# An attention and MLP kernel on one core: batch 0 begun as 512 tokens instead of 256, v cast while it is loaded, and new gates between the two load queues

## The chip, the core and the metric

The kernel runs on one core of a Trainium2 chip. The metric is the device time of one execution in microseconds (us), lower is better. TensorE is called PE here (PEld is its loading of weights), VectorE DVE, ScalarE ACT, GpSimd POOL and SyncE SP. SP and POOL each issue loads and stores of their own queue; a load issued from POOL may change the type on its way (float32 in memory, bfloat16 in SBUF), a load issued from SP does not in this kernel.

## What is computed

Windowed attention with four sink tokens over 4 batches, 8 heads, 768 tokens and 64 elements a head, and behind it two dense layers with a squared ReLU between them:

```python
scores = scale * np.matmul(q, k.transpose(0, 1, 3, 2))
keep = is_sink | in_window            # first 4 tokens, or the last 128 up to one's own
a = softmax(np.where(keep, scores, -1e9))
x = np.matmul(a, v)                   # to [3072 tokens, 512]
h = np.maximum(x @ w_in, 0.0)         # 512 -> 2048
out = (h * h) @ w_out                 # 2048 -> 512
```

Inputs and output are float32; the kernel's matmuls take bfloat16.

## The kernel before, in words

Tokens go in tiles of 128 (six a batch) and slabs of 256 (three a batch). A batch passes through these steps:

- **Loads.** For batches 0 and 1, q and k come over SP's queue as float32 (line 345, tile `qr`), are cast and put in order by `regroup` (lines 208 and 210, tile `qs`, on DVE, POOL or ACT), transposed on PE (line 477, into the PSUM tile `pt`) and copied to `qkT` by DVE and ACT (lines 208 and 206). v comes over SP's queue as float32 (line 361, tile `vf`) and is cast by DVE or POOL (lines 208 and 210, into `v`). For batches 2 and 3 (`NATURAL`) POOL's queue loads q, k (line 378, tile `qn`) and v (line 388) with the cast in the load, and SP's queue transposes q and k by DMA (line 434).
- **Attention by slab.** PE makes the scores of a pair of heads (line 580, into `ps`), ACT takes the exponential (line 599, into `expm`), DVE multiplies by a mask (line 608), PE multiplies with v and with the sinks' v (line 641, into `po`; `es` and `vs` are the sinks' part), DVE divides (lines 652 and 653, into `xn_sb`). In the first 512 tokens of batch 0 the mask is instead added on PE as a bias before the scores (line 573), since the masks are not built yet.
- **The bridge.** For batches 0 and 1 PE turns x (line 678, into `px`) and ACT or DVE copies it to `xT`; for 2 and 3 a DMA does it (line 664).
- **Layer 1** (`layer1`): 16 matmuls of 128x256 or 8 of 128x512 are one operation (line 701, into `pm`), ACT takes the ReLU (line 710), DVE squares (line 717, into `gT`). **Layer 2** (`layer2`): four matmuls an operation (line 741, into `py`), then a copy (line 206) and a store (line 757).

`w_in` (line 300) and `w_out` (line 307) come in four parts each over POOL's queue, cast in the load.

What stands in which order on each engine isn't written out by hand. The class `Plan` gets every operation with its engines, a cost, what it waits for and a key; it keeps a model of the engines, the pools and the two queues, and takes again and again the operation that can start first (ties by key). `attention` and `layer1`/`layer2` set the keys: `at(g, f0, f1, pools)` spreads the operations of one group of tokens over the stretch f0 to f1 of a batch, `LO` and `HI` do so for batches 2 and 3. `PE_SLACK` and the `margin` of a DMA are corrections of that model. The order that comes out is what runs; the chip's engines then wait for each other by semaphores alone. PSUM holds two pools of two tiles, `att` and `den`.

`GROUPS` tells how many tokens of a batch are loaded and turned together. Before, batch 0 is begun with 256 tokens, then 256, then 256; each load is two pairs of heads (four heads) with rows of 512 bytes. Batch 1 has 512 and 256.

Loads of a queue are chained in the order of the calls at lines 784 to 811. A call's argument `behind` makes the load wait until a load of the other queue has landed (`after_dma`, a semaphore wait on the issuing engine). Before: `w_in` waits for a k load of the second 256 tokens (line 794); the loads of batch 0's third slab wait for `w_out(0)` (line 799); `w_out(2)` waits for v of that slab (line 801); batch 1's loads wait for `w_out(2)` (line 805); the first load of batch 2 waits for a v load of batch 1 (line 382).

While PE has nothing to do at the start, `warm` fills its gaps with matmuls of the identity (line 201).

Of the kernel before, what the change touches and what calls it, by code (L numbers as in the profile page):

```python
# [17 lines left out]
PE_SLACK = 0.219  # L18
# [115 lines left out]
def kernel(  # L134
# [28 lines left out]
    sizes = dict(att=2, den=2, qr=5, qs=6, vf=3, expm=8, r=3, osb=2)  # L163
# [149 lines left out]
    qr_slot, qs_slot, vf_slot = {}, {}, {}  # L313
    qn_t, qn_slot = {}, {}
    qr_t, qs_t, vf_t, ex_t, bank_t = {}, {}, {}, {}, {}
# [3 lines left out]
    GROUPS[0] = [(0, 2), (256, 2), (512, 2)]  # L319
# [3 lines left out]
    def load_qk(b, m0, ti, g, behind=None, yields=()):  # L323


        t0, n = GROUPS[b][g]
        if b == 0 and g < 2:
            half, share = g, (b, m0, ti)
        elif n == 2:
            half, share = m0 // 2, (b, "last", ti)  # L330
        else:
            half, share = None, (b, m0, ti)
        if not half:
            qr_slot[share] = Slot("qr", 2)
        qr_slot[b, m0, ti, g] = qr_slot[share]

        def run(e):
            if half is not None:
                if half == 0:
                    qr_t[share] = work["qr"].tile([128, 2, 4, n * D], FP32, name="qr", tag="qr")  # L340
                t = qr_t[share][:, half]
            else:
                t = work["qr"].tile([128, 4, n * D], FP32, name="qr", tag="qr")
            qr_t[b, m0, ti, g] = t
            return [nc.sync.dma_start(  # L345
                out=t,
                in_=(q, k)[ti][b, 2 * m0:2 * m0 + 4, t0:t0 + 128 * n, :].rearrange(
                    "h (p t) d -> p h (t d)", t=n))]
        ops["qk", b, m0, ti, g] = dma_op("sp", ("qk", b, m0, ti, g), run, 32 * ROW[256 * n], behind,
                                         () if half else [qr_slot[share]], yields)  # L350

    def load_v(b, s, behind=None, yields=()):

        sl = vf_slot[b, s] = Slot("vf", 1)
        for i in range(2):
            t = 2 * s + i

            def run(e, i=i, t=t):
                if i == 0:
                    vf_t[b, s] = work["vf"].tile([128, 2, H, D], FP32, name="vf", tag="vf")  # L360
                return [nc.sync.dma_start(
                    out=vf_t[b, s][:, i], in_=v[b, :, 128 * t:128 * t + 128, :].rearrange("h p d -> p h d"))]
            dma_op("sp", ("v", b, t), run, 8 * 8 * ROW[256], behind if i == 0 else None,
                   [sl] if i == 0 else (), yields)

    def load_natural(b, s, older_values):

        begun = [ops["layer1", b - 2, 0, 0], w_out_op[3]]
        for ti in (1, 0):
            if s == 0:  # L370
                qn_slot[b, ti] = Slot("qr", NT)
            for i in range(2):
                t = 2 * s + i

                def run(e, t=t, ti=ti):
                    if t == 0:
                        qn_t[b, ti] = work["qr"].tile([128, NT, DM], BF16, name="qn", tag="qr")
                    return [nc.gpsimd.dma_start(  # L378
                        out=qn_t[b, ti][:, t, :].rearrange("p (h d) -> p h d", d=D),
                        in_=(q, k)[ti][b, :, 128 * t:128 * t + 128, :].rearrange("h p d -> p h d"))]  # L380
                o = dma_op("pool", ("qk", b, ti, t), run, 64 * 0.032,
                           ("v", 1, 3) if (b, ti, t) == (2, 1, 0) else None,
                           [qn_slot[b, ti]] if t == 0 else ())
                o.after += begun
                o.margin = 2.229
        for t in (2 * s, 2 * s + 1):
            def run(e, t=t):
                return [nc.gpsimd.dma_start(  # L388
                    out=v_sb[b % 2][:, t, :, 0:D],
                    in_=v[b, :, 128 * t:128 * t + 128, :].rearrange("h p d -> p h d"))]  # L390
            o = dma_op("pool", ("v", b, t), run, 64 * 0.032)
            o.after += begun + older_values
            o.margin = 2.229
# [6 lines left out]
    def attention(b, key):  # L400
# [16 lines left out]
        def stage(g, f0, f1, side):  # L417
# [9 lines left out]
            if b in NATURAL:  # L427
                for s in range(NS):
                    for ti in (1, 0):
                        for i in range(2):  # L430
# [8 lines left out]
                            ops["turn", b, ti, t].margin = 4.81  # L439
# [3 lines left out]
            for m in range(0, NP, w) if b not in NATURAL else ():  # L443
                f = 0.08 * m
                m0 = m - m % 2
                bs = Slot(side, 2)
                regs = []
                for ti in (1, 0):
                    sl = qs_slot[b, m, ti, g] = Slot("qs", 1)

                    def regroup(e, m=m, m0=m0, ti=ti):
                        t = qs_t[b, m, ti, g] = work["qs"].tile([128, w, n, 2, D], BF16, name="qs", tag="qs")
                        r = qr_t[b, m0, ti, g][:, 2 * (m - m0):2 * (m - m0) + 2 * w, :]
                        if w == 2:
                            copy(e, t, r.rearrange("p (m h) (t d) -> p m t h d", m=2, d=D))
                        else:
                            copy(e, t[:, 0], r.rearrange("p h (t d) -> p t h d", d=D))
                    who = {"pool": 0.17 + w * n * 0.11}
                    if b or g < 2:
                        who["dve"] = 0.06 + w * n * 0.094  # L460
                    if b == 0 and g == 0:
                        who["act"] = 0.2 + w * n * 0.107
                    regs.append(op(at(f), who, regroup,
                                   after=[ops["qk", b, m0, ti, g]] + prev_tr + begun, takes=[sl],
                                   reads=[qr_slot[b, m0, ti, g]]))
# [38 lines left out]

            for s in range(t0 // 256, last // 256) if b not in NATURAL else ():
                def cast(e, s=s):
                    copy(e, vb[:, 2 * s:2 * s + 2, :, 0:D], vf_t.pop((b, s)))
                ops["cast", b, s] = op(at(0.3 + 0.5 * (256 * s - t0) / (last - t0)),
                                       {"pool": 1.08, "dve": 0.75} if g < 2 else {"pool": 1.08}, cast,
                                       after=[ops["v", b, 2 * s], ops["v", b, 2 * s + 1], c_sinks] + older_values + begun,  # L510
                                       reads=[vf_slot[b, s]])


            if g == 0:
# [7 lines left out]
                def sink_values(e):  # L522
                    for j in range(NP):
# [5 lines left out]
                A["sink_values"] = op(at(0.36), {"pool": 1.4, "dve": 0.9}, sink_values,  # L529
                                      after=older_values + [c_fill, c_sinks, ops["vs_in", b]])  # L530
# [23 lines left out]
            biased = b == 0 and g < 2  # L554
            for s in range(t0 // 256, last // 256):
                fs = 0.36 + 0.5 * (256 * s - t0) / (last - t0)
                norms = []
                for m0 in (0, 2):
# [4 lines left out]
                    def scores(e, ms, s=s, m0=m0, banks=banks):  # L563
# [32 lines left out]
                    for j, m in enumerate((m0, m0 + 1)):  # L596
# [19 lines left out]
                        if biased:  # L616
                            masked.append(ex)
                            continue
                        masked.append(op(at(fm + 0.03), {"pool": 1.3, "dve": 0.7} if s else {"dve": 0.58, "pool": 1.1},
                                         domask, after=[ex, late["masks"]]))  # L620
# [40 lines left out]
                if b in NATURAL:  # L661
                    for t in (2 * s, 2 * s + 1):
# [5 lines left out]
                        o_.margin = 3.168  # L668
# [115 lines left out]
    NATURAL = (2, 3)  # L784
    load_sinks("act", 0)
    for g, m0 in ((0, 0), (0, 2), (1, 0), (1, 2)):
        for ti in (1, 0):
            load_qk(0, m0, ti, g)
        if g:
            load_v(0, m0 // 2)  # L790
    for b in range(1, B):
        load_sinks("sp", b)
    for i in range(4):
        load_w_in(i, ("qk", 0, 2, 1, 1) if i == 0 else None)
    load_w_out(0)
    load_w_out(1)
    for m0 in (0, 2):
        for ti in (1, 0):
            load_qk(0, m0, ti, 2, ("w_out", 0) if m0 == 0 and ti == 1 else None, [("w_out", 1)])
    load_v(0, 2, None, ())  # L800
    load_w_out(2, ("v", 0, 4), [("v", 0, 5)])
    load_w_out(3, None, ())
    for m0 in (0, 2):
        for ti in (1, 0):
            load_qk(1, m0, ti, 0, ("w_out", 2) if m0 == 0 and ti == 1 else None, [("w_out", 3)])
    for m0 in (0, 2):
        for ti in (1, 0):
            load_qk(1, m0, ti, 1, None, ())
    load_v(1, 0, None, ())
# [3 lines left out]
    LO, HI = 0.03, 0.504  # L813
    for b in range(B):
        if b == 0:
            at = attention(0, lambda f: f - 1.0)
            at(0, 0.0, 0.5, ("den", "att"))
            at(1, 0.5, 1.0, ("den", "att"))
            w_in_op[2].follow += [ops["cast", 0, 0]]
            w_out_op[0].follow += [ops["cast", 0, 1]]  # L820
            late["masks"] = op(-0.029, {"pool": 3.0}, build_masks, after=[c_tri, ops["bridge", 0, 1]])
            at(2, 1.0, 0.869, ("att", "den"))
# [4 lines left out]
        else:  # L827
            for i, fb in enumerate(range(0, NFB, 2)):
                layer1(b, b + 0.306 * i / 8, (fb, fb + 1), 0, 512, (0, 1))
        for i, fb in enumerate(range(0, NFB, 4)):  # L830
            if b == 0:
                layer1(b, 0.225 + 0.179 * i / 4, range(fb, fb + 4), 512, 256, (2,))
            else:
                layer1(b, b + 0.306 + 0.167 * i / 4, range(fb, fb + 4), 512, 256, (2,))
        if b + 1 < B:
# [3 lines left out]
            if b == 0:  # L839
                at = attention(1, lambda f: f)  # L840
                at(0, 0.063, 1.0, ("att", "den"))
                at(1, 0.249, 0.449, ("att", "den"))
            else:
                attention(b + 1, lambda f, b=b: b + LO + (HI - LO) * f)(0, 0.0, 1.0, "att")
        for u in range(NS):
            if b == 0 and u < 2:
                layer2(b, u, lambda i, part, u=u: 0.403 + 0.303 * (4 * part + 2 * u + i) / 24, by_part=True)
# [38 lines left out]
```

## Time and profile before

| what | value |
|---|---|
| runs before the change | 226.2 us median of 6 (225.9 to 226.96) |
| the profiled execution's own time | 226.4 us |
| its span | 224.7 us, so 1.7 us lie around it |
| mean granted clock of PE | 0.998 |
| DVE, ACT, POOL busy | 104.3, 115.0, 62.5 us |
| packets of POOL's queue, of SP's queue | 40128 and 46024 |
| HBM read, written | 27.30 MB, 6.29 MB |

The profile is read from its page (busy time by engine, the span in 40 slices, the chain of work that ended last, groups of instructions by line) and from answers of the trace: the chain in order of time, the timeline of an engine, who waited for whom, and the packets of the queues in a stretch. Times in them are microseconds from the start of the span; ns only in groups. "x8" is a count of instructions, and "<-" behind a wait names what ended it.

### The profile page before, as it was taken

What the parts mean: (1) busy time and instruction counts of PE and PEld (TensorE: products, weight loads), DVE (VectorE), ACT (ScalarE), POOL (GpSimd) and SP (SyncE); (2) the same over time, 40 slices, a digit from 0 to 9 for tenths busy, and PEclk for the clock granted to TensorE, in tenths of its full rate; (3) what the DMA queues carried; (4) which work ended last, traced back from release to release, by engine and by line L of the source; (5) the groups of instructions that cost most, each with busy time, mean ns of one, the idle gap of its engine ahead of it and who ended that gap; (6) DMA issues with size and microseconds to landing.
All of it is one profiled execution on the core that took longest, in us unless ns stands there. A gap on an engine that the chain in (4) does not pass through costs nothing.

```text
span 224.7 us, 4571 instructions
## 1 busy us (share of the span) xinstructions
PE 215.5 (96%) x1919; PEld 137.4 (61%) x1941; DVE 104.3 (46%) x190; ACT 115.0 (51%) x130; POOL 62.5 (28%) x97
## 2 busy tenths in 40 slices
PE   7889999999999999999999999999999999999993
PEld 7457996457965796555454645587464555884441
DVE  7573733456774577436372533456444123440010
ACT  2397365517776587287635276665443066551010
POOL 5156416124469955966600000000002000000000
PEclk9999999999999999999999999999999999999999
DMA  5999996999989999999999953000121430000222
GB/s 159 252 202 204 213 222 162 183 312 293 206 238 145 104 205 138 136 139 205 153 131 149 207 148 62 3 0 12 38 100 24 136 120 0 0 0 3 93 95 93
DMA packets 86358, 29.70 MB, mean 132 GB/s; under 512 B 70337, under 2 KB 82881, under 8 KB 86337
## 3 DMA queue, kind: packets, MB, share of 16 engines
q0 software_dynamic: 40128, 8.92, 52.4%
q1 hardware_dynamic: 46024, 20.35, 40.5%
q8 instruction: 15, 0.25, 0.5%
q10 hardware_dynamic: 184, 0.14, 0.2%
q14 instruction: 7, 0.05, 0.1%
HBM read 27.30 MB, written 6.29 MB: 149 GB/s over the span
## 4 chain that ended last, share of the span: by engine, by line
PE 88%; ACT 4%; DMA 3%; DVE 1%; SPq 1%; issue 1%; ACTq 0%
PE pm L701 38%; PE py L741 37%; PE po L641 6%; PE ps L580 4%; DMA qr<-in_q_dram 3%; ACT r L710 2%; PE pt L477 1%; SPq L345 1%; ACT expm L599 1%; PE px L678 1%; DVE qkT L208 1%; ACT qkT L206 1%; PE pk L540 1%; PE ps L573 0%; DVE qs L208 0%
## 5 line engine op out<-in xcount | busy, mean ns | idle before, releaser
L741 PE MATMUL py<-w_out_sb,gT 128*128 128x512 bf16 x364 | 86.6, 379 | 1.2 <-issue 0.2
L701 PE MATMUL pm<-xT,w_in_sb 128*128 128x256 bf16 (+1 forms) x576 | 87.0, 308 | 0.7 <-ACT r L710 0.6
L701 PEld LDWEIGHTS <-w_in_sb 128*128 128x128 bf16 x576 | 62.9, 114 | 21.4 <-issue 2.1
L710 ACT ACTIVATE r<-pm 128x1024 bf16<-128x1024 f32 x48 | 49.2, 1025 | 32.9 <-PE pm L701 26.4
L741 PEld LDWEIGHTS <-gT 128*128 128x128 bf16 x384 | 35.4, 98 | 38.5 <-issue 1.4
L599 ACT ACTIVATE expm<-ps 128x1024 bf16<-128x1024 f32 (+1 forms) x48 | 43.3, 953 | 22.6 <-PE ps L580 21.4
L717 DVE TENSOR_TENSOR gT<-r 128x1024 bf16<-128x1024 bf16 x48 | 34.1, 711 | 43.7 <-ACT r L710 43.7
L608 DVE TENSOR_TENSOR expm<-expm,mask 128x1024 bf16<-128x1024 bf16 (+1 forms) x37 | 25.0, 682 | 16.4 <-ACT expm L599 15.8
L206 ACT ACTIVATE osb<-py 128x1024 f32<-128x1024 f32 x10 | 10.3, 1027 | 24.8 <-PE py L741 17.8
L222 POOL TENSOR_SCALAR_AFFINE_SELECT expm<-expm 128x512 bf16<-128x512 bf16 x4 | 2.4, 635 | 62.6 <-ACT expm L599 59.7
L641 PEld LDWEIGHTS <-expm 128*128 128x128 bf16 x352 | 16.6, 97 | 4.9 <-issue 0.8
L641 PE MATMUL po<-v,expm 128*128 128x65 bf16 x352 | 17.9, 193 | 0.3 <-DVE v L208 0.2
L653 DVE TENSOR_TENSOR xn_sb<-po,rc 128x512 bf16<-128x512 f32 x24 | 16.6, 692 | 0.8
L652 DVE RECIPROCAL rc<-po 128x8 f32<-128x8 f32 x24 | 5.0, 206 | 23.5 <-PE po L641 23.1
L580 PE MATMUL ps<-qkT 64*128 64x128 bf16 (+1 forms) x256 | 14.8, 238 | 0.4
L580 PEld LDWEIGHTS <-qkT 64*128 64x128 bf16 x256 | 8.1, 94 | 10.3 <-issue 8.9
L641 PE MATMUL po<-vs,es 128*128 128x65 bf16 x128 | 13.1, 193 | 0.0
L210 POOL CAST qs<-qr 128x512 bf16<-128x512 f32 x11 | 7.7, 702 | 17.7 <-DMA qr<-in_k_dram 9.6
L208 DVE COPY osb<-py 128x1024 f32<-128x1024 f32 (+2 forms) x3 | 2.3, 781 | 21.0 <-PE py L741 17.9
L378 POOL DMA_DIRECT2D qn<-in_q_dram x12 | 10.7, 903 | 4.5 <-DMA qn<-in_k_dram 4.4
L388 POOL DMA_DIRECT2D v<-in_v_dram x12 | 10.7, 898 | 3.9 <-DMA qn<-in_q_dram 3.9
L641 PEld LDWEIGHTS <-es 128*128 128x128 bf16 x128 | 11.7, 97 | 0.0
(51 smaller groups left out, 111.3 us busy)
## 6 DMA issues: line engine op xcount, KB each, us to landing
out_dram<-osb SPq DMA_DIRECT2D x11, 512.0 KB, 3.2
vf<-in_v_dram SPq DMA_DIRECT2D x12, 256.0 KB, 5.7
qr<-in_k_dram SPq DMA_DIRECT2D x8, 256.0 KB, 5.1
qr<-in_q_dram SPq DMA_DIRECT2D x8, 256.0 KB, 4.9
w_in_sb<-in_moe_w_in_dram POOLq DMA_DIRECT2D x4, 512.0 KB, 8.5
w_out_sb<-in_moe_w_out_dram POOLq DMA_DIRECT2D x4, 512.0 KB, 8.3
qn<-in_k_dram POOLq DMA_DIRECT2D x12, 128.0 KB, 11.0
qn<-in_q_dram POOLq DMA_DIRECT2D x12, 128.0 KB, 11.1
```

What stands on the lines that cost most here:

```text
L206: nc.scalar.activation(out=dst, in_=src, func=AF.Copy)
L378: return [nc.gpsimd.dma_start(out=qn_t[b, ti][:, t, :].rearrange("p (h d) -> p h d", d=D), in_=(q, k)[ti][b, :, 128 * t:128 * t + 128, :]. ...
L388: return [nc.gpsimd.dma_start(out=v_sb[b % 2][:, t, :, 0:D], in_=v[b, :, 128 * t:128 * t + 128, :].rearrange("h p d -> p h d"))]
L580: nc.tensor.matmul(ps[:, h2, o:o + w], lhsT=qkT_sb[r, m, 1, c, :], rhs=qkT_sb[r, m, 0, qb:qb + w // 128, :], start=(i == 0 and not biased) ...
L599: nc.scalar.activation(out=x[:, :, o:512], in_=bank_t["s", b, s, m][:, :, o:512], func=AF.Exp, scale=scale)
L608: nc.vector.tensor_mul(x[:, :, o:512], x[:, :, o:512], mk[:, :, o:512])
L641: nc.tensor.matmul(pv[:, i, h2, :], lhsT=lhsT, rhs=rhs, start=(n_ == 0), stop=(n_ == len(mms) - 1))
L653: nc.vector.tensor_tensor(out=xn_sb[:, 2 * s:2 * s + 2, 128 * m0:128 * m0 + 256].rearrange("p i (j h d) -> p j i h d", j=2, d=D), in0=pv[: ...
L701: nc.tensor.matmul(pm[:, i, :], lhsT=w_in_sb[:, fb // 4, kb, fb % 4:512:4], rhs=xT[:, c0 // 256:(c0 + cw) // 256, kb, :], start=(kb == 0), ...
L710: nc.scalar.activation(out=r, in_=bank_t.pop(tag), func=AF.Relu)
L717: (nc.vector if e == "dve" else nc.gpsimd).tensor_mul(gT_sb[c0 // 512][:, fbs[0]:fbs[0] + n, c0 % 512:c0 % 512 + cw], r, r)
L741: nc.tensor.matmul(pm[:, i, :], lhsT=gT_sb[t // 4][:, fb, 128 * (t % 4):128 * (t % 4) + 128], rhs=w_out_sb[:, fb, :], start=(fb == 0), sto ...
```

## The change

What it does, by the order in which instructions then stand on the engines:

- Batch 0 is loaded and turned as 512 tokens and then 256 (`GROUPS[0]`), in place of 256, 256 and 256. The first 512 come in eight loads of one pair of heads each, still 256 KB, with rows of 1024 bytes.
- v of batches 0 and 1 goes over POOL's queue straight into `v`, cast in the load. The tile `vf` and the six casts of it are gone. Four loads of v of batch 0 stand on POOL's queue ahead of `w_in`, and the first of them waits for the first pair's q.
- The gates: `w_in` waits for nothing; `w_out(2)` waits for a k load of batch 0's third slab, and v of that slab stands behind it; batch 1's loads wait for that v; v of batch 1 waits for a k load of batch 1's last slab; the gate of batch 2's first load is gone.
- `sink_values` of batch 0 goes to POOL alone, that of batch 1 waits for the bridge of batch 0's second slab.
- The keys and the corrections of the model are other numbers, so that the order on the engines changes: on PE all eight pairs' scores, the four multiplications with v and both bridges of batch 0's first 512 tokens now stand ahead of the first `layer1`, and its 128 matmuls follow in one run; the transposes of batch 0's third slab follow directly on them. In batches 1 to 3 the pieces of attention, layer 1 and layer 2 are interleaved in another order. The number of PE's matmuls that compute something is the same.

```diff
-PE_SLACK = 0.219
+PE_SLACK = 0.334
...
-GROUPS[0] = [(0, 2), (256, 2), (512, 2)]
+GROUPS[0] = [(0, 4), (512, 2)]
...
-    def load_qk(b, m0, ti, g, behind=None, yields=()):
+    def load_qk(b, m0, ti, g, pairs=2, behind=None, yields=()):
...
     def load_v(b, s, behind=None, yields=()):
-        sl = vf_slot[b, s] = Slot("vf", 1)
-        for i in range(2):
-            t = 2 * s + i
-            def run(e, i=i, t=t):
-                if i == 0:
-                    vf_t[b, s] = work["vf"].tile([128, 2, H, D], FP32, name="vf", tag="vf")
-                return [nc.sync.dma_start(
-                    out=vf_t[b, s][:, i], in_=v[b, :, 128 * t:128 * t + 128, :].rearrange("h p d -> p h d"))]
-            dma_op("sp", ("v", b, t), run, 8 * 8 * ROW[256], behind if i == 0 else None,
-                   [sl] if i == 0 else (), yields)
+        for t in (2 * s, 2 * s + 1):
+            def run(e, t=t):
+                return [nc.gpsimd.dma_start(
+                    out=v_sb[b % 2][:, t, :, 0:D],
+                    in_=v[b, :, 128 * t:128 * t + 128, :].rearrange("h p d -> p h d"))]
+            o = dma_op("pool", ("v", b, t), run, 1.15, behind if t == 2 * s else None, (), yields)
+            o.after.append(c_fill)
+        ops["cast", b, s] = o
...
                 o = dma_op("pool", ("qk", b, ti, t), run, 64 * 0.032,
-                           ("v", 1, 3) if (b, ti, t) == (2, 1, 0) else None,
+                           None,
                            [qn_slot[b, ti]] if t == 0 else ())
                 o.after += begun
-                o.margin = 2.229
+                o.margin = 1.661
...
-                A["sink_values"] = op(at(0.36), {"pool": 1.4, "dve": 0.9}, sink_values,
-                                      after=older_values + [c_fill, c_sinks, ops["vs_in", b]])
+                A["sink_values"] = op(at(0.36), {"pool": 1.9, "dve": 1.4} if b else {"pool": 1.9}, sink_values,
+                                      after=older_values + [c_fill, c_sinks, ops["vs_in", b]] +
+                                      ([ops["bridge", 0, 1]] if b == 1 else []))
...
-    for g, m0 in ((0, 0), (0, 2), (1, 0), (1, 2)):
+    for m in range(NP):
         for ti in (1, 0):
-            load_qk(0, m0, ti, g)
-        if g:
-            load_v(0, m0 // 2)
+            load_qk(0, m, ti, 0, 1)
     for b in range(1, B):
         load_sinks("sp", b)
+    load_v(0, 0, ("qk", 0, 0, 0, 0))
+    load_v(0, 1)
     for i in range(4):
-        load_w_in(i, ("qk", 0, 2, 1, 1) if i == 0 else None)
+        load_w_in(i, None if i == 0 else None)
...
-            load_qk(0, m0, ti, 2, ("w_out", 0) if m0 == 0 and ti == 1 else None, [("w_out", 1)])
+            load_qk(0, m0, ti, 1, 2, ("w_out", 0) if m0 == 0 and ti == 1 else None, [("w_out", 1)])
+    load_w_out(2, ("qk", 0, 2, 1, 1), [("qk", 0, 2, 0, 1)])
     load_v(0, 2, None, ())
-    load_w_out(2, ("v", 0, 4), [("v", 0, 5)])
     load_w_out(3, None, ())
...
-            load_qk(1, m0, ti, 0, ("w_out", 2) if m0 == 0 and ti == 1 else None, [("w_out", 3)])
+            load_qk(1, m0, ti, 0, 2, ("v", 0, 5) if m0 == 0 and ti == 1 else None, [("w_out", 3)])
...
-    load_v(1, 0, None, ())
+    load_v(1, 0, ("qk", 1, 2, 1, 1), [("qk", 1, 2, 0, 1)])
...
-    LO, HI = 0.03, 0.504
+    LO, HI = 0.12, 0.624
...
-            at(0, 0.0, 0.5, ("den", "att"))
-            at(1, 0.5, 1.0, ("den", "att"))
-            w_in_op[2].follow += [ops["cast", 0, 0]]
-            w_out_op[0].follow += [ops["cast", 0, 1]]
-            late["masks"] = op(-0.029, {"pool": 3.0}, build_masks, after=[c_tri, ops["bridge", 0, 1]])
-            at(2, 1.0, 0.869, ("att", "den"))
+            at(0, 0.0, 1.0, ("den", "att"))
+            late["masks"] = op(0.006, {"pool": 3.0}, build_masks, after=[c_tri, ops["bridge", 0, 1]])
+            at(1, 0.2, 0.725, "att")
...
-                at(0, 0.063, 1.0, ("att", "den"))
-                at(1, 0.249, 0.449, ("att", "den"))
+                at(0, 0.179, 0.751, ("att", "den"))
+                at(1, 0.369, 0.369, ("att", "den"))
```

## Prediction

> **What bounds the kernel.** The page first, then the chain in order of time, then who waits for whom, then the packets of the queues. The page:
>
> ```profile
> span 224.7 us, 4571 instructions
> ...
> PE 215.5 (96%) x1919; PEld 137.4 (61%) x1941; DVE 104.3 (46%) x190; ACT 115.0 (51%) x130; POOL 62.5 (28%) x97
> ...
> PEclk9999999999999999999999999999999999999999
> ```
>
> PE is busy for 215.5 of 224.7 us at full granted clock, and the change leaves its useful matmuls as they are. So only the 9.2 us in which PE is idle, and the time at the start that is filled with warm-up matmuls, can move. By stretches of the trace PE is idle for 1.5 us in the first 6 us, 1.1 from 6 to 12, 0.8 from 12 to 18, about 2.1 from 30 to 215, and 4.0 at the end (last matmul, copies, store), which the change does not touch. The start, then, is where most can be won or lost. Its chain:
>
> ```profile
> 9.84 0.43 DVE qs L208
> ...
> 13.22 2.33 ACT expm L599 x3
> ...
> 15.98 0.45 PE pt L477 x8
> ...
> 19.06 1.87 PE pm L701 x16
> 20.93 1.45 PE po L641 x48
> 22.38 1.75 PE pm L701 x16
> 24.13 0.45 PE px L678 x8
> 24.57 10.48 PE pm L701 x96
> ```
>
> The reader is to see that loads and casts lead to 9.84, ACT's exponentials to 15.5, and that from there PE works without a hole until the 128 matmuls of batch 0's first layer 1 are done at 24.57 + 10.48 = 35.05 us. That point is the yardstick: everything ahead of it is the same work before and after the change. 96 of these matmuls took 10.48 us, 0.109 each, so 128 take 13.97. After the change all 128 stand behind the second bridge, so the yardstick becomes the end of that bridge plus 13.97.
>
> **Part 1, the new start.** Loads of q and k became usable as follows (timeline of DVE; in brackets how long it had sat idle, and for what):
>
> ```profile
> 7.14 0.43 DVE L208 CAST qs<-qr 128x512 bf16<-128x512 f32 x1 [1.10 <-DMA qr<-in_k_dram]
> ...
> 8.94 0.43 DVE L208 CAST qs<-qr 128x512 bf16<-128x512 f32 x1 [0.77 <-DMA qr<-in_k_dram]
> 9.84 0.43 DVE L208 CAST qs<-qr 128x512 bf16<-128x512 f32 x1 [0.47 <-DMA qr<-in_q_dram]
> ```
>
> The second load was cast at 5.61, the third at 7.14, the sixth at 9.84: 0.9 us a load of 256 KB. Now eight loads with 1024-byte rows are needed before the last pair of heads is complete. The queues' packets (6 to 8 us with 512-byte rows and some v; 48 to 52 us with batch 1's 1024-byte rows):
>
> ```profile
> DMA packets 1403, 0.61 MB, mean 307 GB/s; under 512 B 372, under 2 KB 1403, under 8 KB 1403
> DMA packets 1548, 1.40 MB, mean 351 GB/s; under 512 B 46, under 2 KB 1547, under 8 KB 1547
> ```
>
> 262 kB at 351 GB/s is 0.75 us a load against 0.85. From 5.61 five steps of 0.75 put the seventh load (the last k) at 9.4. Quickest: 0.72 a step, 9.2. Slowest: the gap to 7.14 stays and four steps are 0.9, 10.7.
>
> The Trainium skill, "DMA: Bandwidth & Descriptors", section "Specifications", says that descriptors of 512 bytes already reach line rate. It speaks against this step: by it the longer rows gain nothing, the steps stay 0.9, the seventh load comes at 10.1, and the sum below ends 0.7 us higher, at no change. The 307 and 351 GB/s disagree with it, mixed rows and all.
>
> On ACT that last k is one of two casts, and what then stands in its order is one copy of `qkT`, eight exponentials and the sinks' one. Rows by form: casts and copies 0.60, exponentials 0.81 (128x768) and 1.02 (128x1024), sinks 0.39. Sum: 0.60 + 0.60 + 4 x 0.81 + 4 x 1.02 + 0.39 = 8.9 us, and about 0.2 between them: 9.4 + 9.1 = 18.5 (before, the last exponential ended at 19.33 + 1.04 = 20.37). PE can feed it: transposes (0.45 a pair), bias and scores (0.65 to 0.85 a pair and slab) are shorter than the exponentials they release. Then 12 of the last 24 `po` matmuls 0.4, reciprocal and division with their waits 1.1 (22.38 to 23.46 before), the second `px` 0.45: bridge done at 20.5, yardstick 20.5 + 14.0 = 34.5, **0.55 us earlier**. With the bounds of the loads: 34.3 to 35.8, from 0.75 earlier to 0.75 later. What the old order had hidden is lost: 32 `pm` matmuls (3.5 us) covered waits for DVE's division, and nothing covers them now.
>
> **Part 2, v and w_in on POOL's queue.** Before, w_in was held back:
>
> ```profile
> POOL w_in_sb L300 <- DMA qr<-in_k_dram: 4.3, 1, 4.3
> SPq L345 <- DMA w_out_sb<-in_moe_w_out_dram: 21.9, 2, 13.8
> ```
>
> It was issued at 13.0 and its first matmul ran at 18.98, 5.9 us later. Now POOL makes four `vs` (0.44 each, from 4.1 to 5.9), by then q of the first pair has landed (5.61), issues four v loads (0.89 each, as rows L388) to 9.5, and then w_in. From 68 to 72 us POOL's queue moved 4670 packets, 1024 a load: 0.88 us a load, no slower than the issues. So w_in(0) lands at 9.5 + 5.9 = 15.4, needed at 20.5: hidden by 5.1 us. The other end: from 72 to 76 us only 1327 packets went, 3.1 us a load; four loads then cost 4 x 2.2 = 8.9 more, w_in(0) at 24.3, 3.8 us late. I take 0.88, since no DMA transpose runs this early, as did from 68.64 on. Parts 1 to 3 of w_in land within 2.6 us of each other and are used 3.5 us apart: no wait.
>
> SP's queue waited 21.9 us for w_out in two places. With w_in 3.5 us earlier, the third slab's loads start at 26.0 in place of 29.55, and the later of the two casts that its first transposes need, at 35.31 to 35.92 on POOL, moves to 32.4. This is needed: its transposes now stand right behind the 128 matmuls (34.5), ahead of the `py` matmuls that came first before. Cost nothing with 2.1 us of cover; if the queue gains nothing, 1.4 us.
>
> **Part 3, what stands behind the gates.** `w_out(2)` on POOL waits for a k load (about 31), then v of the slab and `w_out(3)` follow. v lands at about 38.5 and is used after 8.6 us of `py`, transposes and scores, near 43.5; `w_out(2)` near 44: nothing. Batch 1's loads wait for that v: 38.5 against 43.32. v of batch 1 waits on POOL behind four casts that need PE's transposes, so its six issues run from about 53.1 to 58.5. Landing: from 63.73 to 72 us POOL's queue had moved 5778 packets, 5.6 loads, the sixth of which was issued at 68.3; with 1.5 us to its semaphore that is 5.4 us from issue, so 63 here. PE's order needs it near 65.7 (I summed the order from 34.5 on with the same rows; the third slab comes first). Nothing, with 2.7 us of cover; the median landing of such loads late in the run was 12.2 us, which would make it 4.1 us late.
>
> **Part 4, casts gone, keys.** Six casts leave (four on DVE, 0.69 to 1.03; two on POOL, 1.05). PE waited for one by 0.2 us, inside the start already counted. Elsewhere DVE is idle at 54%: nothing. The reordering moves the two waits of `pm` for ACT's `r` (0.28 and 0.34 us at 60 and 63) to one place, where I find 0.45. I take 0.15 us won; bounds 0.6 either way, what those two waits sum to.
>
> **Sum.** 226.4 - 0.55 - 0.15 = 225.7 for an execution like the profiled one. That one lies 0.2 above the median, so **225.5** as a median, 0.7 us or 0.3% under 226.2. A measurement of this kernel can tell about 0.2% (0.45 us) from no change.
>
> **Rivals.**
>
> - *Hidden anyway*: the seventh load comes at 10.1 or later. The start then ends near 35.1 and PE's total decides: 226.2. For it: the third load took 1.5 us behind the second, and PE had no hole from 15.5 on before. Against: the rates above.
> - *PE alone decides the start*: if ACT also begins its exponentials before the last k and the small waits go, the bridge is done at 19.8 and both waits for `r` vanish: 226.2 - 1.25 - 0.35 = 224.6. Against: ACT's order puts its cast ahead of all exponentials.
> - *Slower, w_in behind v*: it decides from 2.2 us a v load on, where the 5.1 us of cover are used up. POOL's queue took 52.4% of 16 engines' span; less its eight weight loads at 2.7 us, that is 2.7 us for each of 36 loads. At that price w_in(0) lands at 15.4 + 4 x 1.8 = 22.6, the yardstick is 36.6, and the kernel takes 226.2 + 1.5 = 227.7. For it: q and k still come when v begins. Against: packets in that stretch overlapped (share 231% from 68 to 72), so the share overstates it.
> - *Slower, batch 1's v late*: up to 4.1 us, 229 to 230.
>
> That the change does not do what it says I exclude: the order of instructions shows the loads, gates and the missing casts.
>
> **Numbers.** Forecast 0.42 (its own range 224.9 to 226.2), hidden 0.16, PE alone 0.14, w_in behind v 0.18, batch 1's v 0.10. Faster: 0.14 and 0.34 of the forecast's 0.42, 0.48. Same: the other 0.08 and 0.12 of hidden, 0.20. Slower: 0.28 and the 0.04 of hidden that the slowest loads take past 226.65, 0.32. The range must leave out no more than 0.2: it ends at 224.3 under "PE alone" and at 227.7 at the price of w_in behind v, leaving out half of that case and batch 1's.
>
> **What would show it.** Casts of the last pair at 9.4 to 10.2; ACT's exponentials without holes to about 18.5; layer 1's 128 matmuls from 20.5 to 34.5 with no wait for w_in; transposes of the third slab without a wait; v of batch 1 landed by 63. A PE wait for w_in near 20 us, or for v near 66, makes the prediction wrong.

## The result, and the profile after

The changed kernel took 225.92 us (median of 20 runs, 225.1 to 227.32) against 226.26 for the kernel before (42 runs of its own session): ratio 0.9989, interval 0.9978 to 1.0. Measured a second time it was 226.23 against 226.19, ratio 1.0001 (0.9987 to 1.0014). So it is between 0.2% faster and 0.1% slower. The forecast, 225.5, was 0.4 us too low by the first measurement and 0.7 by the second; the range held. The first profiled execution took 225.56 us (span 223.9), a lucky one: the profiles of before and after differ by 0.84 us, the medians by 0.34 and by nothing.

The page after:

```profile
span 223.9 us, 4586 instructions
PE 215.9 (96%) x1932; PEld 138.7 (62%) x1952; DVE 103.3 (46%) x192; ACT 115.8 (52%) x131; POOL 64.8 (29%) x99
```

PE does the same work and the span is shorter by 0.8. Where this came from is seen in two marks that divide the same work in both kernels: the yardstick (end of batch 0's 128 layer-1 matmuls) and the start of the last 96 `py`, behind which all is alike. The first columns are times; "start won" and "middle won" are the lead over before at the yardstick, and what was added between the marks.

| kernel | yardstick | last 96 `py` begin | start won | middle won |
|---|---|---|---|---|
| before | 35.05 | 200.32 | | |
| after, first trace | 35.00 | 199.23 | 0.05 | 1.04 |
| after, second trace | 34.89 | 199.95 | 0.16 | 0.21 |

The start, which should have won 0.55, won almost nothing. Its chain in order of time (start, duration, what; the first trace):

```profile
9.67 0.63 ACT qs L206
...
16.93 1.20 PE po L634 x36
18.13 0.45 PE po L201 x8
18.58 0.73 PE po L634 x24
19.30 0.45 PE px L671 x8
19.75 0.56 PE px L201 x10
20.31 0.53 PE px L671 x8
...
20.86 14.13 PE pm L694 x128
```

The rows of L201 are warm-up matmuls. The planner puts them into PE's order where its own model sees a gap, and they run whether the chip has that gap or not: here PE had none from 16.93 to 20.86. The timeline of ACT:

```profile
12.77 0.60 ACT L206 ACTIVATE qkT<-pt 128x512 bf16<-128x512 bf16 x1 [0.16 <-DVE qkT L208]
...
15.24 2.80 ACT L590 ACTIVATE expm<-ps 128x768 bf16<-128x768 f32 x3
19.79 2.11 ACT L206 ACTIVATE xT<-px 128x1024 bf16<-128x1024 bf16 x2 [1.74 <-PE px L671]
```

The last exponential ended at 18.04, before the predicted 18.5, and before the 36 `po` did (18.13). So the trace shows nothing that held the next 24 `po` but the 8 warm-up matmuls in front of them. The start was lost behind 18.04. The forecast gave 0.4 us to 12 `po`; it took 1.26 to the end of all 24 at 19.30 (0.09 for the rest of the 36, 0.45 for the warm-ups, 0.73 for the 24). Division and the second `px` then took 1.54, against 1.55 in the forecast. The forecast also left out the copy of slab 0's `px` to `xT`, the first half of ACT's last row (19.79 to 20.81). That copy ended 0.03 before the second `px` did (20.84), so the first `pm`, at 20.86, stood behind both about equally.

What the loads did ahead of this is read from DVE's timeline, before and then after. A row that ends with a DMA in brackets had waited for that load.

```profile
4.07 1.18 DVE L524 TENSOR_TENSOR vs<-vs_in,head_rows 32x130 bf16<-32x130 f32 x4 [0.29 <-DMA vs_in<-in_v_dram]
5.28 0.76 DVE L208 CAST qs<-qr 128x512 bf16<-128x512 f32 x2
```

```profile
4.37 0.57 DVE L208 CAST qs<-qr 128x512 bf16<-128x512 f32 x1 [0.23 <-DMA qr<-in_q_dram]
6.08 0.43 DVE L208 CAST qs<-qr 128x512 bf16<-128x512 f32 x1 [1.14 <-DMA qr<-in_k_dram]
6.93 0.45 DVE L208 CAST qs<-qr 128x512 bf16<-128x512 f32 x1 [0.43 <-DMA qr<-in_q_dram]
...
8.86 0.43 DVE L208 CAST qs<-qr 128x512 bf16<-128x512 f32 x1 [0.69 <-DMA qr<-in_q_dram]
...
10.52 0.43 DVE L208 CAST qs<-qr 128x512 bf16<-128x512 f32 x1 [0.64 <-DMA qr<-in_q_dram]
```

Before, the second of the casts from 5.28 on (at 5.61) had not waited for its load: DVE was busy with `vs` until 5.25, and that q had landed at 4.73, 3.4 us after its issue. After, the second load's cast began at 4.37 and the seventh's, on ACT, at 9.67.

The middle shows the other finding. At the same instruction, the `py` in front of the first third-slab `pm`, the second trace is 0.71 us behind the first, though it had led by 0.11 at the yardstick. First trace, then second (both the chain in order of time):

```profile
52.06 0.89 PE pt L476 x16
...
53.01 0.81 PE py L734 x3
```

```profile
43.03 8.23 DMA qr<-in_k_dram
...
51.29 0.43 DVE qs L208
51.71 0.61 DVE qkT L208
...
52.35 0.61 ACT qkT L206
...
53.00 0.67 PE pt L476 x8
...
53.72 0.81 PE py L734 x3
```

In the first, 16 transposes of batch 1 run without a hole. In the second, batch 1's k of pairs 2 and 3 lands at 51.26, and the second eight wait for it by 0.58 us. This load stands on an edge, and executions of one kernel fall on either side.

### The profile page after: what moved, and what is told of

It reads as the page before. It is cut to its first block, busy times and chain, and to the rows that moved or that the text cites. A ratio compares the mean times of both kernels' runs of the same rounds, so it can differ in the third digit from the quotient of the medians.

```text
span 223.9 us, 4586 instructions
## 1 busy us (share of the span) xinstructions
PE 215.9 (96%) x1932; PEld 138.7 (62%) x1952; DVE 103.3 (46%) x192; ACT 115.8 (52%) x131; POOL 64.8 (29%) x99
## 4 chain that ended last, share of the span: by engine, by line
PE 92%; DMA 3%; ACT 2%; SPq 1%; issue 1%; DVE 0%; ACTq 0%
PE pm L694 38%; PE py L734 37%; PE po L634 7%; PE ps L571 5%; DMA qr<-in_k_dram 3%; PE pt L476 2%; PE px L671 1%; SPq L348 1%; PE ps L564 1%; ACT expm L590 1%; PE pk L531 1%; ACT r L703 0%; ACT qs L206 0%; PE px L201 0%; PE ps L201 0%
## 5 line engine op out<-in xcount | busy, mean ns | idle before, releaser
L710 DVE TENSOR_TENSOR gT<-r 128x1024 bf16<-128x1024 bf16 x48 | 33.2, 692 | 49.9 <-ACT r L703 49.8
L206 ACT ACTIVATE osb<-py 128x1024 f32<-128x1024 f32 x9 | 9.2, 1023 | 30.8 <-PE py L734 30.7
L208 DVE COPY osb<-py 128x1024 f32<-128x1024 f32 (+2 forms) x4 | 3.6, 890 | 19.0 <-PE py L734 15.9
L390 POOL DMA_DIRECT2D v<-in_v_dram x12 | 10.7, 918 | 4.7 <-DMA qn<-in_q_dram 4.7
L210 POOL CAST qs<-qr 128x512 bf16<-128x512 f32 x6 | 4.1, 692 | 26.5 <-DMA qr<-in_q_dram 14.8
L361 POOL DMA_DIRECT2D v<-in_v_dram x12 | 10.9, 923 | 0.6 <-DMA qr<-in_k_dram 0.6
L380 POOL DMA_DIRECT2D qn<-in_k_dram x12 | 10.8, 927 | 0.2 <-issue 0.2
```

Of the source, the lines that this page charges most:

```text
L361: return [nc.gpsimd.dma_start(out=v_sb[b % 2][:, t, :, 0:D], in_=v[b, :, 128 * t:128 * t + 128, :].rearrange("h p d -> p h d"))]
L380: return [nc.gpsimd.dma_start(out=qn_t[b, ti][:, t, :].rearrange("p (h d) -> p h d", d=D), in_=(q, k)[ti][b, :, 128 * t:128 * t + 128, :]. ...
L390: return [nc.gpsimd.dma_start(out=v_sb[b % 2][:, t, :, 0:D], in_=v[b, :, 128 * t:128 * t + 128, :].rearrange("h p d -> p h d"))]
L710: (nc.vector if e == "dve" else nc.gpsimd).tensor_mul(gT_sb[c0 // 512][:, fbs[0]:fbs[0] + n, c0 % 512:c0 % 512 + cw], r, r)
```

## Experiments

From e5 on, all kernels but the last have the changed kernel's order written down and held fixed (a list of operations with their engines in place of the planner's choice; for e12 that of e2). Without that, the planner answers any change of a cost with another order for the rest of the program.

**e1, the changed kernel again** (no edit).

> The changed kernel as it is, once more. Its first trace put the end of batch 0's 128 layer-1 matmuls (the yardstick) at 35.00 us (before: 35.05) and the last layer-2 matmul at 219.97 (before: 221.07), yet the medians differ by 0.34 us only. Theory 'the trace is typical': yardstick within 0.2 us of 35.0 again, layer 2 over at 219.8 to 220.3, and the difference to the median lies after it (tail over 3.93 us) or in the profile's luck; time 225.5 to 226.0. Rival 'the start varies from execution to execution with the loads': yardstick more than 0.3 us from 35.0.

226.23 us, yardstick 34.89. The start is steady within 0.1; what varies is the middle, by 0.8 (the chain above).

**e2, old keys.**

```diff
-    PE_SLACK = 0.334;  LO, HI = 0.12, 0.624;  at(0, 0.179, 0.751, ...)
+    PE_SLACK = 0.219;  LO, HI = 0.03, 0.504;  at(0, 0.063, 1.0, ...)
...
```

> The changed kernel with the planner's keys, margins and slack of the kernel before (new start, loads with cast and gates stay). Theory A, the 1.05 us won between 35 and 88 us comes from the order that the new keys give: this kernel loses it, two or more waits of layer 1 for ACT's r come back, time 226.5 to 227. Theory B, it comes from earlier loads and absent casts, not from keys: time 225.7 to 226.1, as after. In either, the yardstick stays at 34.9 to 35.2.

227.41 us, ratio 1.0039 (1.0014 to 1.0064); yardstick 34.84, last 96 `py` from 200.59. The time lies on theory A's side, beyond its 226.5 to 227, but the reason is not A's: the waits of `pm` for `r` that before had (0.28 and 0.34) do not come back. PE waits for something else (engine, for what: us in total, times, longest):

```profile
PE po L634 <- DMA v<-in_v_dram: 1.1, 1, 1.1
```

The old order needs v of batch 1 at 65.2, and it landed at 66.3. The forecast's fourth rival, batch 1's v late, is real with the old keys.

**e3, the kernel before with the new keys** (e2's edit the other way, on the kernel before; only batch 0's third slab, which before is a group of its own, keeps its keys).

> The kernel before (256-token start, v loaded by the hardware queue and cast by engines) with the keys, margins and slack of the changed one. Theory A (order): the order alone wins, 225.2 to 225.8, yardstick at 35.0 to 35.3, one wait of layer 1 for r at most. Theory B (loads and casts): no gain or a loss, 226.1 to 227, since the third slab's loads come as late as before.

229.05 us, ratio 1.0135 (1.0104 to 1.0166). The new keys alone win nothing. As theory B says, the third slab's loads come as late as before (from 29.57 us, before 29.55), but the loss is not there: its transposes still stand behind seven `py` and begin at 36.56 (before 36.78). From 60 to 90 us PE was busy 26.93 us where before had 29.10; `po` waited there for DVE's product with the mask (1.4 us in three waits) and `py` for ACT's `r` (0.8). Why these waits come with the new keys, no run separates.

**e4, the kernel before with v cast in POOL's loads, and the new gates.** Its start has 256 tokens, and its keys are the old ones.

```diff
-    load_v(0, m0 // 2)                              # SP's queue, float32, cast by DVE or POOL
+    load_v(0, 0, ("qk", 0, 0, 0, 0)); load_v(0, 1)  # POOL's queue, ahead of w_in
...
```

> The kernel before with one part of the change alone: v of batches 0 and 1 cast in loads on POOL's queue, with the new gates; start of 256 tokens and old keys stay. Theory A (order): nothing won, 226.0 to 226.6. Theory B (loads and casts): most of the gain, 225.2 to 225.8, third slab's transposes and batch 1's attention without waits. A third outcome: v now lands later for the first 256 tokens than from the hardware queue, PE waits for v near 16 us, and the time is 226.8 to 228.

234.42 us, ratio 1.0351 (1.0326 to 1.0376). The yardstick is 35.10, as before, though PE waited 1.7 us for v (two waits). The rest was lost behind it, where the planner made another order with waits for ACT (2.4 us for `expm`, 1.7 for `r`). It says little on theory B, and was the reason to hold the order fixed.

**e5, `px` of slab 0 ahead of the last 24 `po`.**

```diff
-PE: po x24 (slab 1), px (slab 0), px (slab 1), pm ...
+PE: px (slab 0), po x24 (slab 1), pm x16, px (slab 1), pm ...
-ACT: xT<-px (slab 1)
+DVE: xT<-px (slab 1)
```

The written order also leaves out the 8 and the 10 warm-up matmuls (L201 in the chain above) that stood ahead of the last 24 `po` and of the second `px`. The same holds for e9 and e11.

> The changed kernel with its whole order written down and held fixed, and one thing moved: slab 0's px goes ahead of the last 24 po of slab 1, the px of slab 1 behind the first 16 pm, its copy to DVE. Theory C, what the prediction left out of the bridge is the copy of px to xT (1.02 us on ACT, 19.79 to 20.81 in the trace after): 128 pm may then begin at about 20.1, and the yardstick is 20.1 + 14.0 + 0.45 = 34.5 instead of 35.0. Rival, the start ends where ACT's last exponential and DVE's divisions end, wherever px stands: 34.9 to 35.1. On the time: 225.6 to 225.8 if the 0.5 us stay; 226.1 to 226.3 if they are given back where batch 1's k load lands at 51.3.

225.76 us, ratio 0.9974 (0.9959 to 0.9988); last 96 `py` from 198.70. Its chain:

```profile
18.26 0.52 PE px L671 x6
...
18.81 1.03 ACT xT L206
...
19.88 1.91 PE pm L694 x16
21.79 0.45 PE px L671 x8
22.24 12.23 PE pm L694 x112
```

`pm` follows the copy of `xT` at once, and the yardstick is 34.47, as theory C had it. But not all of the 0.53 belongs to the edit. A mark for how far loads and casts had come is the start of the three copies of `qkT` that DVE makes behind the last q's cast (10.86 in the first trace of after). From there to the yardstick are 24.14 us in both traces of after, and 24.12 to 24.15 in e6, e8 and e10, which keep after's order there. Here the copies began at 10.70, and 23.77 us lie behind: 0.37 us are the edit's, 0.16 came ahead of it. What in the edit won the 0.37 (the place of `px`, the copy on DVE, or the absent warm-ups) is not separated; after's order without the warm-ups was not tried. In e2, whose planner put three warm-ups fewer into this stretch, it is 24.03 us, 0.11 less.

**e6, ACT's two casts of k on DVE** (`regroup` of k, pairs 2 and 3: "act" becomes "dve").

> The changed kernel in its own fixed order, but the two casts of k that ACT did (7.60 and 9.67 us) on DVE. Theory 'ACT's chain behind the last k sets the start' (the prediction's step): ACT's first exponential 0.6 us earlier or more, the last ends at 17.0 to 17.5, yardstick 34.2 to 34.6. Rival 'the landing of the last k and q and DVE's queue set it': DVE now casts both last tensors one behind the other, the last exponential ends at 18.0 to 18.6, yardstick 35.0 to 35.5. Time 225.7 or 226.2 to 226.7.

225.75 us, ratio 0.998 (0.9965 to 0.9995). ACT's timeline and PE's chain:

```profile
8.57 2.83 ACT L590 ACTIVATE expm<-ps 128x768 bf16<-128x768 f32 x3
12.14 0.60 ACT L206 ACTIVATE qkT<-pt 128x512 bf16<-128x512 bf16 x1 [0.75 <-DVE qkT L208]
```

```profile
20.23 14.13 PE pm L694 x128
```

The exponentials begin 1.64 us earlier, yet ACT then stands idle for 0.75 us until DVE has copied the last pair's `qkT`. The yardstick, 34.36, looks like a win for theory "ACT's chain". But the last q's cast began at 9.88, and 24.48 us lie between, as in both traces of after (10.52 to 35.00, 10.41 to 34.89), and as in e8 (10.69 to 35.16) and e10 (10.66 to 35.15). The start hangs on the landing of the last **q**, through DVE's cast and three copies, not on the last k and ACT. The theory falls. Whether the move won anything is not settled, since the interval overlaps that of the changed kernel.

**e7, batch 1's loads without their gate on v.**

```diff
-    load_qk(1, m0, ti, 0, 2, ("v", 0, 5) ...)
+    load_qk(1, m0, ti, 0, 2, ("qk", 0, 2, 0, 1) ...)
```

> The changed kernel in its own fixed order, but batch 1's first q and k loads wait for the third slab's q load instead of for the last v of batch 0 (41.57). Theory D, that gate is what makes batch 1's second k land at 51.3, on the edge, and costs 0 to 0.7 us from execution to execution: loads start at about 34.5, k has landed by 46, no transpose of batch 1 waits, 225.3 to 225.7 with a smaller spread. Rival: the q and k loads now share the DMA engines with w_out and v of batch 0, v lands after 44.5, and PE waits for it or for w_out(2) by 0.5 to 3 us: 226.5 to 229.

232.5 us, ratio 1.0283 (1.0259 to 1.0307). The rival, and worse than it had said. Waits of PE, the chain, and the queues' packets from 42 to 46 us (packets, MB, share of 16 engines):

```profile
PE po L634 <- DMA v<-in_v_dram: 5.1, 2, 3.1
```

```profile
36.30 13.44 DMA v<-in_v_dram
```

```profile
q1 hardware_dynamic: 966, 0.96, 87.8%
q0 software_dynamic: 966, 0.12, 46.3%
```

Both queues got the same number of packets, 966. v's are 128 bytes as written, those of q and k 1024, so v moved an eighth of the bytes, and landed 12.2 us after its issue (median of its two loads). With the gate it had the engines alone (2220 packets of POOL's queue from 38 to 42 us, none of SP's), took 5.7 and had landed by 41.57. The Trainium skill, "DMA: Bandwidth & Descriptors", section "Queues, rings and completion order", says that a DMA engine takes turns among the queues packet by packet. The equal counts fit such turns; they do not show how many rows go in one turn. What the rows show by themselves is the cost to the queue with small rows. This is what the gates of the change are worth: 6 us at this one.

**e8, four more loads of v ahead of `w_in`.**

```diff
+    for i in range(4):
+        load_again(i)     # v of batch 0 into batch 1's buffer, POOL's queue
```

> The changed kernel in its own fixed order with four additional dummy loads of v on POOL's queue ahead of w_in (0.88 us each by the trace after, 3.5 us in all; they go to a buffer that batch 1's v overwrites). If the cover of w_in is as the trace after says (landed at about 17.5, needed at 20.86): w_in(0) at 21.0, a wait of 0.2 us at most, but third-slab loads behind w_out(0) 3.5 us later, and a wait of 1.0 to 1.5 us of its transposes at 35: 227.0 to 227.7. If a v load in that queue costs more than its issue (the prediction's rival, 2.2 us or more each): w_in(0) at 26 or later, wait of 5 us or more near 21, 231 or more. If it costs nothing on the path: 226.2.

228.04 us, ratio 1.0091 (1.0071 to 1.0111); `w_in` was issued from 13.38 (after: 9.75). PE's waits:

```profile
PE pt L476 <- DVE qs L208: 1.8, 2, 1.5
...
PE pt L476 <- POOL qs L210: 1.0, 1, 1.0
```

No wait for `w_in`, and none near 21 us. The first part of `w_in` landed 7.3 us after its issue, at 20.7, and was needed at 21.03, so its cover held 3.6 us of additional loads with about 0.35 to spare. Of the first row, 1.47 us stand at 8.34, in the start, and they cost it little: the yardstick is 35.16. The loss comes behind it, where SP waits for `w_out(0)`. The third slab's loads start at 31.06 in place of 27.64, its transposes wait (the second row, 1.0, as forecast), and batch 1's k, later too, costs again: behind the first trace of after the kernel is by 0.16 us at the yardstick, by 1.50 at the eight `py` that follow the third slab's first scores (39.44) and by 2.42 at the three `py` ahead of the first third-slab `pm` (55.43). The time lies a little above the 227.0 to 227.7 I gave it.

**e9, e5 and e6 together.**

> The changed kernel in fixed order with both moves at the start: px of slab 0 first (yardstick 34.47 by itself) and ACT's two casts on DVE (34.36 by itself). Theory 'the two shorten different parts of one chain' (exponentials begin earlier; what follows the last one is shorter): yardstick 33.8 to 34.0, time 225.2 to 225.4. Rival 'both shorten the same part': 34.3 to 34.5 and 225.6 to 225.8. Third: the yardstick falls to 33.9 but PE then waits for the third slab's casts or batch 1's k, which the loads set: 225.6 to 225.9.

225.38 us, ratio 0.9953 (0.9932 to 0.9973): 1.1 us below the kernel before in the same session, better than both kernels, and the best time of the study. The time is that of "different parts of one chain", but its trace does not show why. The profiled execution was the slowest of its twelve (226.38). Its yardstick is 34.52, 23.76 us behind DVE's three copies, as in e5 alone; so in this trace the casts on DVE added nothing, which is "the same part". And it had this in its chain and its waits:

```profile
30.00 6.30 DMA qr<-in_q_dram
```

```profile
PE ps L571 <- ACT qkT L206: 0.7, 1, 0.7
```

The third slab's last q landed at 36.3, and what the start had won was given back there, as in the third reading (without its yardstick of 33.9). Eight of the twelve runs lie from 225.2 to 225.72, four at 226.05 or above. Its interval overlaps those of e5 and e11, so the lead over these is not settled.

**e10, v ahead of `w_out(2)`.**

```diff
-    load_w_out(2, ("qk", 0, 2, 1, 1), ...); load_v(0, 2, None, ())
+    load_v(0, 2, ("qk", 0, 2, 1, 1), ...); load_w_out(2, None, ())
```

> The changed kernel in fixed order, with the two loads of v of the third slab ahead of w_out(2) on POOL's queue, so that the gate of batch 1's loads, which is that v, opens earlier. Theory D, the landing of batch 1's k (50.6 in one trace of the changed kernel, 51.3 with a wait of 0.6 in the other) is set by that gate: SP's loads start at 40.9 to 41.3 instead of 41.6 to 42.0, k lands by 50.5, no transpose of batch 1 waits, 225.6 to 225.9. Rival: w_out(2), now 1.8 us later in its issue, lands after its first matmul (44.7), PE waits 0.5 us or more: 226.5 or more. If neither shows: 226.2.

226.08 us, ratio 0.9982 (0.9964 to 1.0). The loads of batch 1 did start 1.5 to 1.9 us earlier (40.11), and yet:

```profile
41.26 9.99 DMA qr<-in_k_dram
51.27 0.43 DVE qs L208
```

k landed at 51.25, as in the second trace of after, and a transpose of batch 1 waited again (0.3 us). Theory D falls as I put it: the gate is not what dates this load. From 46 to 50 us in the trace after, SP's queue alone takes 101.6% of the 16 engines, which fits loads that wait for each other; this is argued, not tested.

**e11, e9 and e10 together.**

> The two moves at the start and v ahead of w_out(2), in fixed order. If the start's gains add and the gate is what gives them back: 224.9 to 225.2, yardstick 33.8 to 34.0, no wait for batch 1's k. If the gate has no part in it: as the kernel with the two moves alone.

225.71 us, ratio 0.9969 (0.9948 to 0.9991): no gain over e9 is seen (the intervals overlap), so nothing speaks for the earlier gate. The yardstick is 35.21. Here DVE worked without a wait for a load from 7.58, when the second pair's q had landed (7.56), to the three copies at 11.43; with ACT's two casts in its queue it came to the last q's only at 10.86. From the copies on it is 23.78 us, as in e5 and e9. k of batch 1 came in time (49.5), and the middle won 1.04.

**e12, e2 without the gate of batch 1's v.**

```diff
-    load_v(1, 0, ("qk", 1, 2, 1, 1), ...)
+    load_v(1, 0, None, ...)
```

> The changed kernel with old keys (227.41), its order held fixed, with one gate taken away: v of batch 1 no longer waits for batch 1's last k load. Theory B (the loads, not the keys, won the time between 35 and 88; the old keys lose only because they need batch 1's v at 65.2, where it lands at 66.3): POOL issues v about 1.5 us earlier, the 1.1 us wait goes, 226.2 to 226.4. Rival: v now shares the queues with q and k of batch 1 and both come as late: 227 or more.

225.71 us, ratio 0.9966 (0.995 to 0.9982), where e2 had 1.0039: 1.7 us for one gate. POOL issued v from 53.85 (e2: 55.52) and the wait for it fell from 1.1 to 0.3 us. So the old keys with one gate less are not slower than the changed kernel (their interval and that of its first measurement touch). Yardstick 34.72, last 96 `py` from 199.37: 0.62 us won in the middle without the new keys. That is theory B's reading, that the middle is won by loads and casts; its number is not met, since the time lies below its 226.2 to 226.4 and the wait for v is shorter but not gone.

## Why the prediction was right, and where it was not

The forecast named the right size (no more than a few tenths) and put it in the wrong place.

- **Part 1, start, 0.55 us: measured 0.05 and 0.16.** The last k was cast at 9.67 and 9.57, near the 9.4 given, but by luck. I took 5.61 for the landing of the second load before, when it had landed at 4.73 and waited for DVE; and the step of 0.75 us held only from 6.08 to 7.60 (two steps), before packets of v came. From the second load's cast at 4.37 the five steps took 1.06 each, and the two errors nearly cancelled. The 512-byte rule of the Trainium skill ("DMA: Bandwidth & Descriptors", section "Specifications") that I had weighed against it gave 10.1. The rates speak mildly against that rule: 327 GB/s with 512-byte rows (before, 3 to 4 us), 336 to 357 with 1024 (after, 5 to 8 us). ACT ended 0.46 earlier than I had it. Two things failed. First, the sum behind ACT: the 0.4 us for `po` were 1.26, since all 24 were left and 8 warm-up matmuls stood ahead of them. So "bridge done at 20.5" was 20.86, in spite of ACT, and 128 `pm` took 14.13, not 13.97, since the first 16 of them take longer (1.87 of 14.10 in the row that I had shown). These two differences, 0.52, are the missing 0.5. The copy to `xT` was left out as well; it ended with the second `px`, so by itself it added next to nothing here, but would have held `pm` had PE been faster. e5 shows that order, copy and warm-ups together are worth 0.37. Second, I followed the seventh load and not the eighth: the start is the cast of the last q plus 24.48 us in five traces. That q came 0.3 late against my step of 0.75 (10.15). From 9 to 10 us POOL's queue moved 960 packets of v and SP's 103, after 387 in the microsecond before. SP's queue had only some 113 packets of this stretch left at 9.0; at the 352 a microsecond that it moved from 6 to 7 they would have taken 0.3 us, and they took just over 1, so I estimate up to 0.7 us. So v ahead of `w_in` probably costs the start something through the last q, not through `w_in`; this is argued from e7's rows, and a kernel with v behind the last q was not tried.
- **Part 2, `w_in` hidden: right,** with less cover than I gave: the first part landed 7.8 us after its issue, not 5.9, at 17.55, and was needed at 20.86, so 3.3 us and not 5.1. e8, with 3.6 us of loads more, just held. The rival "w_in behind v" is out, with its 2.2 us a load. The third slab's loads started at 27.64 and 27.42 (26.0 given), its transposes had no wait at 35.0, as predicted. e8 and e9 show that this cover is thin.
- **Part 3, gates: the step "`w_out(2)` (about 31)" failed.** Its k load landed at 34.3, so the v behind it landed at 41.57 and not 38.5, and batch 1's loads began 3.1 us later than I said. I costed that at nothing; it is nothing in one trace and 0.6 to 0.7 us in the other, and e10 shows that an earlier gate did not mend it. v of batch 1 was issued 2 us late as well, and its last load, issued at 59.5, took 6.5 us and landed at about 66.0, not by 63 as the signs had it. My 5.4 us for such a load was counted from packets; the load of the kernel before from which I took it had needed 8.1 us to its landing. With the new keys PE needs v only at 67.0 (I had 65.7) and does not wait: 1.0 us of cover, not 2.7. The cover came from the keys: e2, which needs v at 65.2, pays 1.1 us.
- **Part 4, casts gone and keys, 0.15 us: measured 1.04 where every load is in time** (first trace, e5, e11; 0.94 in e6) **and 0.21 in the second trace.** I looked for it in the order. e2 and e12 show that the waits for `r` go with the old keys too, and e12 that 0.62 are won with them. So most of it comes with the loads and the casts; which of these two, no run separates. The new keys pay for the late v.
- **Sum.** 0.55 + 0.15 was 0.7. Measured at the last 96 `py`: 0.05 + 1.04 = 1.09 in the lucky trace (0.84 at the end of the span, as the stretch behind the last matmul took 3.9 us, before 3.65), 0.16 + 0.21 = 0.37 in the other; between nothing and 0.34 in the medians. That the total came near is luck in part: the start's 0.55 was not there, and the middle gave up to 1.04 where I had 0.15. "Hidden anyway" (226.2) is where the second measurement lies, though not for its reason: the last q and PE's work behind it hold the start, and in that trace k of batch 1 takes back what the middle wins. "PE alone" is out: the start never reached 34.

## What to carry to other kernels

Sum a chain to the first instruction that can really start, with copies out of PSUM and with all that the engine's own order still holds ahead of it, warm-up matmuls too. Follow every load that the chain joins, not only the one that looks last, and take a load's landing from a cast that waited for it, not from one that was itself held up. Before two queues run at once, compare their rows: here both moved the same number of packets, and the queue with small rows paid. One gate was worth 6.3 us, and another one cost 1.7. Where a load lands on an edge, a single profile can differ from the next by more than the change is worth, so take a second trace before tenths of a microsecond are explained.

## What the runs showed of the hardware

- Two queues that both had work got 966 packets each in 4 us, at 1024 and 128 bytes a packet; the loads with the small rows took 12.2 us from issue to landing, alone 5.7.
- Four more cast loads on POOL's queue, 0.88 to 0.92 us each to issue, delayed what stood behind them by about that (`w_in` 3.6 us, the third slab's loads 3.4).
- Warm-up matmuls took their time from PE where it had no gap: 8 took 0.45 us and 10 took 0.56, in a stretch in which PE was never idle.
- The landing of the last of eight loads varied from execution to execution by 0.8 us: its cast began from 9.88 to 10.69 in the nine traces in which DVE had waited for it, with the same loads ahead of it on its queue. In the five of them that keep after's order up to the yardstick, the start followed it one for one. Casts that began early lasted longer in some traces (0.58 us in e5, else 0.43); the cause is open.
